# A written order for all five queues from tile 1 on, with attention and weight sums cut into small pieces

## The chip, the cores and the metric

The kernel runs on one core of a Trainium2 chip. TensorE (PE) multiplies matrices into PSUM, VectorE (DVE), ScalarE (ACT) and GpSimd (POOL) work on elements, and SyncE (SP) issues nearly all DMA transfers here. Each engine works through its own queue in order and waits at an instruction until what it needs is there. The metric is the device time of one execution in microseconds; smaller is better.

## The reference

```python
scores = scale * np.matmul(q, k.transpose(0, 1, 3, 2))      # q, k, v: 8 batches, 8 heads, 576 x 64
mask = (rel >= 0) & (rel < window)                           # window = 64
scores = np.where(mask, scores, -1000000000.0)
scores = scores - np.max(scores, axis=-1, keepdims=True)
attn = np.exp(scores)
attn = attn / (np.sum(attn, axis=-1, keepdims=True) + 1e-09)
x = np.matmul(attn, v)                                       # then laid out as 4608 tokens x 512
rms = np.sqrt(np.mean(x * x, axis=-1, keepdims=True) + 1e-06)
xn = x / rms * rms_g
g = xn @ w_gate                                              # 512 x 1536
silu = g * (1.0 / (1.0 + np.exp(-g)))
val = xn @ w_val
return (silu * val @ w_out).astype(np.float32)               # 1536 x 512
```

All arrays are fp32. The kernel keeps the accuracy by splitting each fp32 operand of the large products into an f16 high part and an f16 low part and adding three f16 products (high by high, high by low, low by high).

## The kernel before

The 4608 tokens are nine tiles of 512 (tile 0 to 8). A batch has 576 tokens, so batch b fills the end of one tile and most of the next; its attention is done while the tile before is multiplied. Batches 0 and 1 belong to the start (tile 0, where the weights are also widened and split); the change concerns what follows, batches 2 to 7 and tiles 1 to 8.

**Tiles.** In tiles 1 and 2, `expert_in` makes 24 groups of 12 matmuls of 512 columns (`pg`, `pv`: gate and value), each pair followed by a tanh (L850, ACT), two multiply steps (L851, L852, DVE), the high part (L853, ACT) and the low part (L854). `expert_out` then makes `po`, 24 chunks of 6 matmuls, and `store` copies it out (`ot`, L1046, ACT). From tile 3 on (`FIRST7`) a product of 2 by 2 blocks is done with seven products instead of eight: `seventh` runs product p of chunk c (12 matmuls of 256 columns, L927), at slot 7c + `PLACE[p]` of its tile's 66 slots. The other slots hold `po` chunks. Some of the seven need sums of the activations (`combine`, L785 to L797: `xn`, `wt`, `t`) and of the weights. `snap` (L942, ACT) copies product 1, 5 or 6 away so that later products may add to it on DVE (L980, L983, L987); product 7's sum is made in the copy of product 5 (`p5`, a piece of `wt` in SBUF).

**Weight sums.** `prepare` makes the weights' sums once, in twelve calls, each a block of DVE, ACT, POOL and SP instructions (L878 to L892); the results lie in DRAM (`sevens`), and `load_sevens` (L909, SP) brings a chunk's back before it is used, into a ring of three, after the last product that read the buffer.

**Attention.** A batch has four pairs of heads. For a pair: q and kv are loaded (L325, L340, L353, L354, SP), 36 matmuls give the scores (L396), nine masks with a running maximum (L409, DVE), nine exps with sums (L412, ACT), a reciprocal (L439, L440), a scaling in two multiplies (L373, POOL), a way to DRAM and back that regroups the rows (`via`, L377 and L381, SP), a transpose (L384, L385, DVE), 36 matmuls with the values (L520), copies to `xb` (L577), a square (L583, ACT) and a sum `ssq` (L588). After four pairs the root of the mean square is taken. For batches 0 and 1, `inverse_roots` reduces with columns of one (`tot`, L685), does 11 DVE steps on 128x5 numbers and spreads them with matmuls (`broadcast`, `rb`, L727). From batch 2 on, `roots_of_all` multiplies `ssq` with a matrix of ones (`tot`, L712) and does the same 11 DVE steps on 128 x n numbers, once for each of two pieces. `normalise` then scales `xb` (L752, DVE) and makes `xn` for two tiles.

**What sets the order.** The program is written as a sequence of half-steps, 32 to a tile; events have a time in half-steps and are written when the sequence gets there. `visit(n)` writes the scores of pair n with its whole softmax and the values of pair n-2 at one point (`VISITS`, then every 8 half-steps); the scaling follows 1.5 half-steps later, the transpose 6, and the loads come 7 half-steps before the scores. Tile's scheduler then places each engine's instructions by a simulated timeline of its own, with priorities from the order of writing; only on PE, from chunk 3 of tile 1, does `group()` bind each group to the one written before it. PSUM is in several small pools (`ps_mi`, `ps_x`, `ps_mo` and others) until tile 3, and one pool of eight banks from there.

Of the kernel before, what the change touches and what calls it, by code (L numbers as in the profile page):

```python
# [58 lines left out]
def tile_window_attention_moe(
# [25 lines left out]
    in_order = {"on": False}  # L85

    @contextmanager
    def group():

        if not in_order["on"]:  # L90
            yield
            return
        last = next(x for x in reversed(nc.cur_bb.bb.instructions) if x.engine == nc.tensor.engine)
        with tc.issue_after(last):
            yield
# [434 lines left out]
    def attention(b):  # L530
# [12 lines left out]
        def score(hp, g, first=None):  # L543
            qk = qs[hp], pairs[hp][0]
            if b < TB:
                soft[hp, g] = scores(b * NPAIR + hp, g, qk)
            elif g == 0:
                scores_of_pair(b * NPAIR + hp, qk, first)

        def moved(hp):  # L550
            p, m, rs = whole[b * NPAIR + hp]
            move(b * NPAIR + hp, m, p, rs)

        def turned(hp):
            p, m, _ = whole.pop(b * NPAIR + hp)
            turn(p, m)
            soft[hp, 0] = soft[hp, 1] = p
# [4 lines left out]
        def values(hp, g, xp=None):  # L562
# [19 lines left out]
            if x2e == "a":
                nc.scalar.activation(x2, xb[:, hp, :], AF.Square)  # L583
            else:
                (nc.vector if x2e == "v" else nc.gpsimd).tensor_tensor(x2, xb[:, hp, :], xb[:, hp, :], ALU.mult)
            if hp:
                add = nc.vector if (E('ADD', 'ppvppv')[3 * b + hp - 1] == 'v' if b < 2 else hp == NPAIR - 1) else nc.gpsimd
                add.tensor_tensor(ssq, ssq, x2, ALU.add)  # L588
# [120 lines left out]
    def roots_of_all(b, ssq, a, z):  # L709

        tot = x_bank(f"tot_{b}_{a}")[:, : z - a]
        nc.tensor.matmul(tot, lhsT=ones, rhs=ssq[:, a:z], start=True, stop=True)  # L712
# [501 lines left out]
```

## Time and profile before

| | us |
|---|---|
| median of three runs (1052.85 to 1056.49) | 1053.8 |
| the profiled execution | 1056.1 |
| its span, first to last instruction | 1054.3 |
| PE busy | 972.0 |
| DVE, ACT, POOL busy | 655.8, 507.1, 338.6 |

The mean granted clock of PE is 0.971 of full speed. Times in the profile count from the start of the span. The first product of each tile starts at 58.8 (tile 0), 211.7, 338.4, 454.5, 557.0, 662.1, 770.7, 875.8 and 961.9 us (tile 8). Tiles 1 to 6 have attention beside them, tiles 7 and 8 have none. A row such as "PE pv L802 <- DVE th L851" says that PE, about to write `pv` at line 802, had stood idle until DVE had written `th` at line 851. "L802 PE MATMUL ... [5.44 <-DVE th L851]" puts the same wait before one instruction. PEld is the loading of weights into PE and overlaps with PE. The ends of matmuls are modelled and overlap (a row of 0.38 us is followed by the next after 0.215), so starts are the better ruler.

### The profile page before, as it was taken

The numbers are of one execution on the slowest core, as the hardware profiler recorded it, in microseconds if no ns is written. First come the engines' busy times: TensorE is split into PE (matmuls) and PEld (weight loads), VectorE is DVE, ScalarE is ACT, GpSimd is POOL, SyncE is SP. The second block draws the span as 40 slices with busy tenths as digits, with TensorE's granted clock in tenths as the row PEclk, the third lists the DMA queues.
The fourth block names the chain that finished last, engine by engine and source line by source line (L and its number), as shares of the span: only waits on it lengthen the run. The fifth ranks groups of instructions, "written<-read, shape, count | busy, mean of one in ns | idle before, by whom it ended". The sixth has DMA issues, their size and how long they took to land.

```text
span 1054.3 us, 20343 instructions
## 1 busy us (share of the span) xinstructions
PE 972.0 (92%) x7740; PEld 629.6 (60%) x7751; DVE 655.8 (62%) x1713; ACT 507.1 (48%) x1303; POOL 338.6 (32%) x367
## 2 busy tenths in 40 slices
PE   7789989997989899989898999899989899999998
PEld 5544534553434344478656874687468757866875
DVE  5688856288779634846575766666666566531550
ACT  5557875254434343255535653465345525532541
POOL 3425633245424333323223332433243214210210
PEclk9999989998989999999999999999989999999999
DMA  7647851344541656268645774577436532551601
GB/s 282 192 152 221 262 168 50 116 151 136 171 138 58 196 167 202 71 191 278 226 137 155 260 267 140 151 249 256 155 104 208 163 111 82 198 171 35 206 1 40
DMA packets 78241, 171.72 MB, mean 163 GB/s; under 512 B 25792, under 2 KB 38336, under 8 KB 73536
## 3 DMA queue, kind: packets, MB, share of 16 engines
q1 hardware_dynamic: 77568, 169.24, 50.0%
q8 instruction: 61, 1.00, 0.4%
q10 hardware_dynamic: 576, 1.18, 0.3%
q14 instruction: 36, 0.29, 0.1%
HBM read 135.79 MB, written 34.60 MB: 162 GB/s over the span
## 4 chain that ended last, share of the span: by engine, by line
PE 29%; DMA 11%; DVE 10%; ACT 9%; issue 3%; POOL 3%; SPq 2%; DVEq 0%; ACTq 0%; POOLq 0%
PE a L927 17%; DMA pm<-via 6%; DMA via<-pm 5%; ACT pm L412 5%; PE po L802 4%; PE po L804 4%; PE po L803 4%; POOL pm L373 2%; DVE pm L384 2%; SPq L377 1%; DVE th L952 1%; DVE th L953 1%; ACT h L958 1%; ACT th L951 1%; DVE xb L752 1%
## 5 line engine op out<-in xcount | busy, mean ns | idle before, releaser
L927 PEld LDWEIGHTS <-wt 128*128 128x128 f16 x3024 | 297.2, 98 | 75.3 <-issue 32.9
L927 PE MATMUL a<-xn,wt 128*128 128x256 f16 x1728 | 206.3, 275 | 19.7 <-ACT wt L942 7.9
L802 PE MATMUL po<-wt,h 128*128 128x512 f16 (+1 forms) x436 | 164.8, 378 | 0.0
L804 PE MATMUL po<-wt,h 128*128 128x512 f16 (+1 forms) x436 | 164.6, 377 | 0.0
L803 PE MATMUL po<-wt,h 128*128 128x512 f16 (+1 forms) x436 | 164.6, 377 | 0.0
L959 POOL TENSOR_TENSOR h<-th,h 128x512 f16<-128x512 f32 x60 | 69.6, 1160 | 249.2 <-ACT h L958 241.7
L927 PE MATMUL a<-wt,wt 128*128 128x256 f16 x1104 | 134.9, 275 | 9.3 <-ACT s L942 9.3
L412 ACT ACTIVATE pm<-pm,st 128x128 f32<-128x128 f32 (+1 forms) x216 | 83.1, 387 | 24.3 <-DVE st L409 24.1
L373 POOL TENSOR_TENSOR pm<-pm,st 128x1024 f32<-128x1024 f32 (+1 forms) x48 | 59.2, 1252 | 88.0 <-DVE st L440 59.0
L952 DVE SCALAR_TENSOR_TENSOR th<-th,a 128x256 f32<-128x256 f32 x108 | 45.3, 420 | 62.4 <-ACT th L951 61.9
L958 ACT CAST h<-th 128x512 f16<-128x512 f32 x72 | 44.4, 617 | 79.5 <-DVE th L953 79.5
L384 DVE STREAM_TRANSPOSE pm<-pm 128x1024 f32<-128x1024 f32 x24 | 29.9, 1245 | 72.5 <-DMA pm<-via 60.3
L951 ACT ACTIVATE th<-a,hsc 128x256 f32<-128x256 f32 x108 | 51.3, 475 | 44.6 <-PE a L927 25.5
L804 PEld LDWEIGHTS <-h 128*128 128x128 f16 x436 | 43.0, 99 | 49.7 <-issue 2.2
L802 PE MATMUL pv<-xn,wt 128*128 128x512 f16 x144 | 57.6, 400 | 14.4 <-DVE th L851 14.4
L802 PEld LDWEIGHTS <-h 128*128 128x128 f16 x436 | 43.2, 99 | 46.5 <-issue 2.5
L803 PEld LDWEIGHTS <-h 128*128 128x128 f16 x436 | 43.2, 99 | 46.0 <-issue 3.0
L396 PE MATMUL sc<-kv,q 64*64 64x128 f32 (+1 forms) x1056 | 57.5, 300 | 8.4 <-DMA q<-q 5.0
L803 PEld LDWEIGHTS <-wt 128*128 128x128 f16 x296 | 29.6, 100 | 54.3 <-issue 24.1
L854 POOL TENSOR_TENSOR h<-th,h 128x512 f16<-128x512 f32 x30 | 37.4, 1251 | 69.5 <-ACT h L853 60.5
L802 PE MATMUL pg<-xn,wt 128*128 128x512 f16 x144 | 54.8, 381 | 5.3 <-DVE th L852 3.1
L785 ACT CAST xn<-xb 128x192 f16<-128x192 f32 (+7 forms) x33 | 12.9, 423 | 96.4 <-DVE xb L752 96.2
(189 smaller groups left out, 1780.3 us busy)
## 6 DMA issues: line engine op xcount, KB each, us to landing
wt<-sevens SPq DMA_DIRECT2D x36, 1024.0 KB, 5.9
wt<-sevens SPq DMA_DIRECT2D x36, 768.0 KB, 4.4
kv<-kv SPq DMA_DIRECT2D x28, 608.0 KB, 4.7
via<-pm SPq DMA_DIRECT2D x96, 144.0 KB, 2.8
pm<-via SPq DMA_DIRECT2D x24, 576.0 KB, 4.2
q<-q SPq DMA_DIRECT2D x28, 288.0 KB, 3.1
kv<-kv SPq DMA_DIRECT2D x56, 128.0 KB, 4.8
out<-ot SPq DMA_DIRECT2D x27, 256.0 KB, 2.1
```

Of the source, the lines that this page charges most:

```text
L373: nc.gpsimd.tensor_tensor(p[:, :ks, us, :], p[:, :ks, us, :], r, ALU.mult)
L384: nc.vector.transpose(p[:, :, : NBLK - 1, :], m[:, :, : NBLK - 1, :])
L396: nc.tensor.matmul(out.rearrange("p (n c) -> p n c", c=D), lhsT=qt[hd, j * D : (j + 1) * D], rhs=halves[hd, :1, :] if j == 0 else halves[h ...
L412: nc.scalar.activation(part, part, AF.Exp, bias=low, scale=-1.0, accum_out=total)
L802: nc.tensor.matmul(acc, lhsT=lh, rhs=rh, start=first, stop=False)
L803: nc.tensor.matmul(acc, lhsT=lh, rhs=rl, start=False, stop=False)
L804: nc.tensor.matmul(acc, lhsT=ll, rhs=rh, start=False, stop=last)
L927: nc.tensor.matmul(acc[:, i * HT : (i + 1) * HT], lhsT=ws[l][:, kt, :], rhs=b[:, m, kt, :], start=at_start, stop=kt == 1 and j == 2, skip_ ...
L951: nc.scalar.activation(cols, acc[:, :HT], AF.Tanh, scale=th_scale[:, c : c + 1])
L952: nc.vector.scalar_tensor_tensor(cols, cols, 1.0, acc[:, :HT], ALU.add, ALU.mult)
L958: nc.scalar.copy(hh, th)
L959: (nc.vector if c == NC - 1 else nc.gpsimd).tensor_tensor(hl, th, hh, ALU.subtract)
```

## The change

From tile 1 on, one time scale of slots holds everything: 72 slots for tiles 1 and 2 (`LONG`), 66 for tiles 3 to 8 (`SHORT`); a slot is six matmuls of 512 columns or twelve of 256. `at_slot` keeps a sorted list, and `rest_of_tiles` writes what is due before each slot's matmuls. A pair's softmax is no longer one block: scores at slot -14, -4, 8 or 21 of the tile, masks 0.5 apart, exps 0.9 apart, scaling at 10 (in three multiplies instead of two), to DRAM at 12.5, back at 16, transpose at 22, values at slot 12, 22, 34 or 47 of the tile, then square and sum. Loads are written 6 slots before the scores (14 for the first two pairs). `normalise` and `combine` are lists of pieces 0.85 apart. `prepare` is twelve lists of twelve parts, 0.9 apart, one list every 9.6 slots from slot 3 of tile 1. Roots are those of batches 0 and 1 for all batches (`NRB = B`); `roots_of_all` is gone. Product 7's sum goes into the PSUM bank of product 3. The eight-bank pool begins with tile 1. At the end each instruction written after that point is bound to follow the one written before it on its engine, on all five engines.

```diff
-VISITS = (27, 32, 37, 42.5, 47.5)
-MOVED, TURNED = 1.5, 6
+SCORES, VALUES = (-14, -4, 8, 21), (12, 22, 34, 47)
+LOAD, MASK, EXP, SUM, SCALE, AWAY, BACK, TURN = -6, (0.3, 0.5), (1.3, 0.9), 9.7, 10, 12.5, 16, 22
+ROOTS, FIRST, SECOND, PIECE = 50.5, 52.5, 61, 0.85
 FIRST7 = 3
-SLOTS = 66
 PLACE = {1: 0, 5: 2, 2: 3, 6: 4, 3: 6, 7: 8, 4: 12}
-ORDERED = (1, 3)
-PREP0, PREP1 = 34.0, 72.0
+LONG, SHORT = 72, 66
+PREP, PREP_EVERY, PREP_PIECE = 3, 9.6, 0.9
 ST = 2 * NBLK * P - 32
-NRB = 2
...
+NRB = B
...
+    def scale(p, rs):
+
+        for ks, us in ((4, slice(0, 4)), (4, slice(4, NBLK - 1)), (2, slice(NBLK - 1, NBLK))):
...
+    vias = {}
+
+    def away(n, p):
+        vias[n] = dram.tile([P, 4, NBLK * 32], F32, tag="via", name=f"via_{n}", bufs=3)
...
+    def back(n, m):
+        nc.sync.dma_start(out=m.rearrange("p q j c -> p q (j c)"), in_=vias.pop(n))
...
+        parts = [(MASK[0] + MASK[1] * i, partial(mask, u)) for i, u in enumerate(order)]
+        parts += [(EXP[0] + EXP[1] * i, partial(power, u)) for i, u in enumerate(order)]
+        return parts + [(SUM, invert)]
...
+    def attention_slots(b):
+        load_queries, load_keys, score_pair, moves, values, squares, add, roots, normal_parts = attention(b)
+        t0 = tile_start(b - 1)
+
+        def all_of(hp, when):
+            for off, part in score_pair(hp):
+                at_slot(when + off, part)
+            for off, part in moves(hp):
+                at_slot(when + off, part)
+
+        def normal(piece, when):
+            for i, part in enumerate(normal_parts(piece)):
+                at_slot(when + PIECE * i, part)
+
+        for hp in range(NPAIR):
+            s, v = t0 + SCORES[hp], t0 + VALUES[hp]
+            early_by = 14 if b == TB and hp < 2 else -LOAD
+            at_slot(s - early_by, partial(load_queries, hp))
+            at_slot(s - early_by, partial(load_keys, hp))
+            at_slot(s, partial(all_of, hp, s))
+            at_slot(v, partial(values, hp, 0))
+            at_slot(v + 0.4, partial(values, hp, 1))
+            at_slot(v + 1.5, partial(squares, hp))
+            at_slot(v + 2.2, partial(add, hp))
+        at_slot(t0 + ROOTS, roots)
+        at_slot(t0 + FIRST, partial(normal, 0, t0 + FIRST))
+        at_slot(t0 + SECOND, partial(normal, 1, t0 + SECOND))
...
-    def visit(n):
-
-        xp = x_bank(f"x0_{n}")
-        if n in visits:
-            visits[n][0](any_bank(f"s0_{n}") if shared else ps_mi.tile([P, TT], F32, tag="mi", name=f"s0_{n}"))
-        if n - 2 in visits:
-            visits[n - 2][1](0, xp)
-            visits[n - 2][1](1)
...
-        tot = ps_mi.tile([P, TT], F32, tag="mi", name=f"tot_{b}")
+        tot = any_bank(f"tot_{b}") if shared else ps_mi.tile([P, TT], F32, tag="mi", name=f"tot_{b}")
...
-    def roots_of_all(b, ssq, a, z):
-
-        tot = x_bank(f"tot_{b}_{a}")[:, : z - a]
-        nc.tensor.matmul(tot, lhsT=ones, rhs=ssq[:, a:z], start=True, stop=True)
-        m, r, w = (
-            wk.tile([P, TT], F32, tag="t2k", name=f"r{i}_{b}_{a}", bufs=T2K)[:, : z - a]
-            for i in range(3)
-        )
-        inverse_root(m, r, w, tot)
-        return r
...
-            rb = broadcast(b, r, a, z) if b < NRB else roots_of_all(b, ssq, a, z)
...
+            held["rb"] = broadcast(b, r, a, z)
...
+        return [
+            partial(copies, 0), partial(whole_of, 0), partial(copies, 1), partial(whole_of, 1), partial(sums, 0), partial(sums, 1),
+            partial(half, 0, 1), partial(half, 0, 0), partial(half, 1, 0), partial(half, 1, 1), partial(away, 0), partial(away, 1),
+        ]
...
-            p5 = kept.pop((c, 5))
-            nc.vector.tensor_tensor(p5, acc, p5, ALU.add)
-            quad(t, c, 1, 1, p5)
+            w = kept[c, "w"]
+            nc.vector.tensor_tensor(w, acc, kept.pop((c, 5)), ALU.add)
+            quad(t, c, 1, 1, w)
...
+    def rest_of_tiles():
+        def until(when):
+            while timed and timed[0][0] <= when:
+                timed.pop(0)[2]()
+
+        now = 0
+        for t in range(1, FIRST7):
+            for c in range(NC):
+                for i in range(2):
+                    for m in range(2):
+                        until(now)
+                        group_in(t, c, i, m, any_bank)
+                        now += 2
+                if t == FIRST7 - 1 and c % 2:
+                    at_slot(now, partial(load_sevens, c // 2))
+            for k in range(TT // P):
+                for c in range(NC):
+                    until(now)
+                    out_unit(t, k, c)
+                    now += 1
...
+        for slot in range(now, tile_start(NT)):
+            until(slot)
...
-    for n in range(NPAIR * TB, NPAIR * B + 2):
-        at_step(visit_at(n), partial(visit, n))
+    for b in range(TB, NBR):
+        attention_slots(b)
...
+    def prepared(n, when):
+        for i, part in enumerate(prepare(n // 2, n % 2)):
+            at_slot(when + PREP_PIECE * i, part)
+
     for n in range(2 * NC):
-        at_step(PREP0 + (PREP1 - PREP0) * n / (2 * NC), partial(prepare, n // 2, n % 2))
+        at_slot(PREP + PREP_EVERY * n, partial(prepared, n, PREP + PREP_EVERY * n))
...
+    rest_of_tiles()
+    assert not plan and not timed
+    start = next(k for k in reversed(range(len(traced))) if traced[k] is mark) + 1
+    for ins in traced[start:]:
+        if ins.engine in before and ins.engine in WRITTEN(nc):
+            tc.add_manual_dep(
+                ins, before[ins.engine].name,
+                mybir.DependencyInfo(mybir.DependencyClass.NoSync, mybir.DependencyReason.DATA), reason="written order",
+            )
+        before[ins.engine] = ins
```

Three places show the order. First ACT between tiles 5 and 6. `ot_5_k` are the output copies of tile 5, `pm_30` is the softmax of batch 7's third pair, `xb`, `xn` and `wt` belong to the activations' pieces, and `s1_6_0` is the copy of tile 6's first product. Before:

```order
L412 ACTIVATE pm_30_8216,st_30_8217<-pm_30_8216,st_30_8217 128x2x32
L785 CAST wt1_82<-t1_7_128_8119 128x2x224
L785 CAST wt4_85<-xb_6_6971 128x2x224
L412 ACTIVATE pm_30_8216,st_30_8217<-pm_30_8216,st_30_8217 128x4x32 x7
L785 CAST wt4_85<-t0_7_128_8118 128x2x224
L1046 ACTIVATE ot_5_2_8178<-po_5_2_8139,hsc_123 128x512
L412 ACTIVATE pm_30_8216,st_30_8217<-pm_30_8216,st_30_8217 128x4x32
L785 CAST xn_7_8097<-t2_7_128_8120 128x2x224
L577 COPY xb_7_8248<-x0_30_8194 128x320
L577 COPY xb_7_8248<-xp_28_1_8251 128x256
L942 COPY s1_6_0_8294<-a1_6_0_8281 128x512
```

After (`pm_29` is the pair before it):

```order
L1135 ACTIVATE ot_5_2_8055<-po_5_2_7995,hsc_123 128x512
L827 CAST wt0_81<-t3_6_0_8030 128x2x64
L411 ACTIVATE pm_29_8088,st_29_8089<-pm_29_8088,st_29_8089 128x2x32
L827 CAST wt4_85<-t2_6_0_8061 128x2x64
L411 ACTIVATE pm_29_8088,st_29_8089<-pm_29_8088,st_29_8089 128x4x32 x2
L827 CAST xn_7_8043<-xb_6_7137 128x2x224
L827 CAST xn_6_6769<-t4_6_0_8123 128x2x64
L411 ACTIVATE pm_29_8088,st_29_8089<-pm_29_8088,st_29_8089 128x4x32
L1007 COPY s1_6_0_8159<-a1_6_0_8146 128x512
L827 CAST xn_7_8043<-xb_6_7137 128x2x224
L411 ACTIVATE pm_29_8088,st_29_8089<-pm_29_8088,st_29_8089 128x4x32
L827 CAST xn_7_8043<-xb_6_7137 128x2x224
```

Seven exps of a pair in one row become pieces of one or two between the casts, and the third output copy stands ahead of the pair's exps.

Second DVE where batch 3's root is taken, at the end of tile 2: `ssq_3` is the sum of squares, `tot_3` its sum over features. Before:

```order
L588 TENSOR_TENSOR ssq_3_3396<-ssq_3_3396,kv_15_3433 128x576
L854 TENSOR_TENSOR h_2_5_3982<-th_2_11_4110,h_2_5_3982 128x512
L700 TENSOR_SCALAR r0_3_0_4145<-tot_3_0_4143 128x320
L701 TENSOR_SCALAR r1_3_0_4146<-r0_3_0_4145 128x320
L705 TENSOR_TENSOR r2_3_0_4147<-r1_3_0_4146 128x320
L706 SCALAR_TENSOR_TENSOR r2_3_0_4147<-r2_3_0_4147,r0_3_0_4145 128x320
L707 SCALAR_TENSOR_TENSOR r1_3_0_4146<-r2_3_0_4147,r1_3_0_4146 128x320
L705 TENSOR_TENSOR r2_3_0_4147<-r1_3_0_4146 128x320
L706 SCALAR_TENSOR_TENSOR r2_3_0_4147<-r2_3_0_4147,r0_3_0_4145 128x320
```

After:

```order
L894 SCALAR_TENSOR_TENSOR th_2_11_3987<-pv_2_11_3974,th_2_11_3987 128x512
L896 TENSOR_TENSOR h_2_5_3915<-th_2_11_3987,h_2_5_3915 128x512
L611 TENSOR_TENSOR ssq_3_3482<-ssq_3_3482,kv_15_3540 128x576
L744 TENSOR_SCALAR rm_3_4045<-tot_3_4039 128x5
L745 TENSOR_SCALAR rm_3_4045<-rm_3_4045 128x5
L749 TENSOR_TENSOR rm_3_4045<-rm_3_4045 128x5
L750 SCALAR_TENSOR_TENSOR rm_3_4045<-rm_3_4045 128x5
L751 SCALAR_TENSOR_TENSOR rm_3_4045<-rm_3_4045 128x5
```

The eleven steps on 320 columns (and eleven more on 256 that follow later) become eleven on 5 columns.

Third SP in tile 5, at the loads of two pairs. Before:

```order
L909 DMA wt0_81<-sevens3_131 128x4096
L909 DMA wt0_81<-sevens3_131 128x3072
L325 DMA q_26_6722<-q 128x576
L909 DMA wt1_82<-sevens4_132 128x4096
L377 DMA via_23_6104<-pm_23_5987 32x4x288 x3
L340 DMA kv_24_6065<-kv 128x1216
L353 DMA kv_24_6065<-kv 64x512
L354 DMA kv_24_6065<-kv 64x512
L377 DMA via_23_6104<-pm_23_5987 32x4x288
```

After:

```order
L974 DMA wt0_81<-sevens3_131 128x4096
L974 DMA wt0_81<-sevens3_131 128x3072
L318 DMA q_27_7208<-q 128x576
L333 DMA kv_27_7210<-kv 128x1216
L346 DMA kv_27_7210<-kv 64x512
L347 DMA kv_27_7210<-kv 64x512
L974 DMA wt1_82<-sevens4_132 128x4096
L974 DMA wt1_82<-sevens4_132 128x3072
L374 DMA via_26_7324<-pm_26_7043 32x4x288 x4
```

The queries of pair 26 were written long before the keys of pair 24; now q and kv of one pair, 27, stand together behind the weights' sums of chunk 3, and the four transfers of `via` are no longer parted.

More of the change, by code (lines that the diff above doesn't have):

```diff
@@ L83, in any_bank @@
         return shared["banks"].tile([P, TT], F32, tag="bank", name=name)
[L85 to L95, printed above, removed]
     def x_bank(name):
@@ L541, in load_keys, with score, score_pair, moves @@
             pairs[hp] = load_kv(b * NPAIR + hp)
-        def score(hp, g, first=None):
+        def score(hp, g):
             qk = qs[hp], pairs[hp][0]
[L545 to L557, printed above, removed]
+            soft[hp, g] = scores(b * NPAIR + hp, g, qk)
+        def score_pair(hp):
+            n = b * NPAIR + hp
+            first = any_bank(f"s0_{n}") if shared else ps_mi.tile([P, TT], F32, tag="mi", name=f"s0_{n}")
+            return scores_of_pair(n, (qs[hp], pairs[hp][0]), first)
+        def moves(hp):
+            n = b * NPAIR + hp
+            def turned():
+                p, m, _ = whole.pop(n)
+                turn(p, m)
+                soft[hp, 0] = soft[hp, 1] = p
+            return (
+                (SCALE, lambda: scale(whole[n][0], whole[n][2])),
+                (AWAY, lambda: away(n, whole[n][0])),
+                (BACK, lambda: back(n, whole[n][1])),
+                (TURN, turned),
+            )
         def to_keys(hp, g):
@@ L831, in tile_window_attention_moe, with group_in @@
     held = {}
+    def group_in(t, c, i, m, bank):
+        xn = xn_tiles[t]
+        if (t, c) not in hs:
+            hs[t, c] = h_tile(t, c)
+        f = 2 * c + i
+        fs = slice(i * P, (i + 1) * P)
+        hh, hl = hs[t, c][:, 0, i, :], hs[t, c][:, 1, i, :]
+        w = (wg, wv)[m][c]
+        a = bank(f"p{'gv'[m]}_{t}_{f}")
+        for kt in range(NKD):
+            three(a, w[:, 0, kt, fs], w[:, 1, kt, fs], xn[:, 0, kt, :], xn[:, 1, kt, :], kt == 0, kt == NKD - 1)
+        if m == 0:
+            acc_of[t, f] = a
+            return
+        g = acc_of.pop((t, f))
+        th = wk.tile([P, TT], F32, tag="t2k", name=f"th_{t}_{f}", bufs=T2K)
+        nc.scalar.activation(th, g, AF.Tanh, scale=th_scale[:, c : c + 1])
+        nc.vector.scalar_tensor_tensor(th, th, 1.0, g, ALU.add, ALU.mult)
+        nc.vector.scalar_tensor_tensor(th, a, 2.0**-41, th, ALU.mult, ALU.mult)
+        (nc.vector.tensor_copy if t < 2 and E('HHE', 'a' * 24)[12 * t + f] == 'v' else nc.scalar.copy)(hh, th)
+        (nc.vector if t and c == NC - 1 else nc.gpsimd).tensor_tensor(hl, th, hh, ALU.subtract)
@@ L869, in prepare, with copies @@
         at = 8 * TT + 3 * TT * i
-        for j in range(2):
+        r, halves = [], []
+        names = {}
+        def copies(j):
             part = out_of[:, at + TT * j : at + TT * (j + 1)].rearrange("p (k f) -> p k f", k=NKD)
@@ L1174, in tile_window_attention_moe @@
     late = ctx.enter_context(tc.tile_pool(name="late", bufs=1))
-    all_sevens()
-    assert not plan
+    traced = nc.cur_bb.bb.instructions
+    before = {}
+    for ins in traced:
+        before[ins.engine] = ins
+    mark = traced[-1]
+    rest_of_tiles()
[6 more added lines that the diff above has]
+                mybir.DependencyInfo(mybir.DependencyClass.NoSync, mybir.DependencyReason.DATA), reason="written order",
+            )
+        before[ins.engine] = ins
 def kernel(**inputs):
```

291 lines of the change are left out of this document (141 added, 150 removed).

## The prediction

> **What bounds the kernel now.** I read the engine shares first, then a table of busy time by tile, then what PE waited for, then the rows around the waits.
>
> The page's head and first part:
>
> ```profile
> span 1054.3 us, 20343 instructions
> PE 972.0 (92%) x7740; PEld 629.6 (60%) x7751; DVE 655.8 (62%) x1713; ACT 507.1 (48%) x1303; POOL 338.6 (32%) x367
> ```
>
> PE is the bound, so the question is when it stands still or runs slowly. Busy time by stretch, cut where a tile's first product starts (window, length; busy time of PE, PEld, DVE, ACT, POOL; PEclk; DMA share, GB/s). The rows are tiles 1 to 7:
>
> ```profile
> 211.70:338.40 126.70, 113.89 (x805) 55.41 (x802) 104.27 (x248) 54.16 (x165) 52.34 (x51) 0.95 0.43 132
> 338.40:454.50 116.10, 106.44 (x726) 51.86 (x725) 68.40 (x187) 49.78 (x152) 41.24 (x43) 0.98 0.51 162
> 454.50:557.00 102.50, 97.64 (x928) 73.44 (x928) 65.73 (x171) 46.48 (x127) 28.77 (x31) 0.97 0.62 203
> 557.00:662.10 105.10, 97.92 (x942) 72.48 (x941) 68.81 (x194) 53.10 (x155) 34.35 (x38) 1.00 0.61 206
> 662.10:770.70 108.60, 99.75 (x942) 72.94 (x941) 72.61 (x201) 54.14 (x158) 35.04 (x39) 0.98 0.60 196
> 770.70:875.80 105.10, 96.89 (x797) 69.86 (x796) 64.84 (x153) 49.21 (x123) 31.96 (x33) 0.95 0.45 143
> 875.80:961.90 86.10, 86.10 (x649) 63.38 (x648) 37.60 (x71) 34.52 (x62) 18.82 (x16) 1.00 0.44 144
> ```
>
> Tile 7, which has no attention beside it, is full: 86.10 us, clock 1.00. Its 66 slots make one slot 86.10/66 = 1.305 us. Tiles 1 to 6 take 664.1 us together and PE is busy for 612.5 of them, so 51.6 us are gaps. No engine but PE is near full over a tile; DVE in tile 1 comes nearest (104.27 of 126.7). What ended PE's gaps in tiles 1 to 6 (total us, times, longest):
>
> ```profile
> PE pv L802 <- DVE th L851: 10.8, 4, 5.4
> PE a L927 <- ACT s L942: 9.3, 3, 3.6
> PE tot L712 <- DVE ssq L588: 8.2, 4, 4.8
> PE a L927 <- ACT wt L942: 7.9, 7, 3.1
> PE a L927 <- DVE wt L987: 6.0, 4, 3.0
> PE a L927 <- ACT ot L1046: 3.2, 1, 3.2
> ```
>
> These 45.4 us are few, long waits for short steps that stood late in the queue of ACT or DVE. ACT's timeline shows such a queue at the start of tile 3 (start, length):
>
> ```profile
> 449.52 0.39 ACT L412 ACTIVATE pm<-pm,st 128x128 f32<-128x128 f32 x1
> ...
> 453.18 0.67 ACT L583 ACTIVATE ssq<-xb 128x576 f32<-128x576 f32 x1
> 453.75 0.67 ACT L1046 ACTIVATE ot<-po,hsc 128x512 f32<-128x512 f32 x1
> ```
>
> From 449.52 to 453.18 ACT does exps with little between, then a square, and only then the copy that frees the bank PE waits 3.2 us for.
>
> The clock comes on top. Three stretches around gaps:
>
> ```profile
> 254.00:262.00 8.00, 3.85 (x10) 1.34 (x10) 6.79 (x7) 3.83 (x9) 6.65 (x5) 0.62 0.48 135
> 521.00:530.00 9.00, 5.99 (x89) 4.99 (x87) 6.77 (x27) 4.39 (x14) 0.15 (x1) 0.81 0.75 272
> 562.00:568.00 6.00, 3.76 (x29) 2.65 (x28) 1.93 (x5) 5.16 (x13) 4.04 (x5) 1.00 0.39 92
> 258.15 0.58 PE L802 MATMUL pv<-xn,wt 128*128 128x512 f16 x1 [5.44 <-DVE th L851]
> 524.25 1.49 PE L927 MATMUL a<-xn,wt 128*128 128x256 f16 x12 [3.01 <-DVE wt L987]
> 564.67 1.47 PE L927 MATMUL a<-wt,wt 128*128 128x256 f16 x12 [2.24 <-ACT s L942]
> ```
>
> The gaps of 5.44 and 3.01 us come with a lower clock, the one of 2.24 does not. By the tile rows the clock costs (1-0.95)x126.7 + 0.02x116.1 + 0.03x102.5 + 0 + 0.02x108.6 + 0.05x105.1 = 19.2 us.
>
> **What PE must do there.** One pair's scores and values, on PE (start, length):
>
> ```profile
> 444.84 0.27 PE L396 MATMUL s<-kv,q 64*64 64x64 f32 x2
> ...
> 446.60 0.64 PE L520 MATMUL xp<-pm,kv 128*64 128x64 f32 x16
> 447.17 0.39 PE L802 MATMUL po<-wt,h 128*128 128x512 f16 x1
> ```
>
> That is 447.17-444.84 = 2.33 us, 24 times, less one pair's scores (0.95, the start of L520 at 445.79) that fall into tile 0: 55.0. Tiles 1 and 2 have 72 slots, 3 to 6 have 66: 2x72x1.305 + 4x86.10 = 532.3. Roots today are one kind of row and become another:
>
> ```profile
> L712 PE MATMUL tot<-ssq,one 128*128 128x384 f32 (+7 forms) x24 | 8.9, 455 | 8.2 <-DVE ssq L588 8.2
> 192.88 1.17 PE L685 MATMUL tot<-one,ssq 128*128 128x1 f32 x10
> 203.13 1.00 PE L727 MATMUL rb<-ident,rm 128*128 128x128 f32 x8
> 210.26 0.66 PE L727 MATMUL rb<-ident,rm 128*128 128x64 f32 x4
> 194.09 0.16 DVE L700 TENSOR_SCALAR rm<-tot 128x5 f32<-128x5 f32 x1 [4.65 <-PE tot L685]
> 196.08 0.17 DVE L707 SCALAR_TENSOR_TENSOR rm<-rm 128x5 f32<-128x5 f32 x1
> L705 DVE TENSOR_TENSOR r<-r 128x384 f32<-128x384 f32 x6 | 3.3, 558 | 0.2
> ```
>
> 532.3 + 55.0 + 8.9 = 596.2, and with 19.2 for the clock 615.4 against 612.5 measured: the account closes within 3 us.
>
> **The change, part by part.**
>
> 1. Roots as batch 1 has them. PE pays 1.17+1.00+0.66 = 2.83 per batch, 17.0 for six, against 8.9: a loss of 8.1. DVE gets 11 steps in 2.2 us (194.09 to 196.25) for two pieces of 11 steps at up to 0.56: about 10 us of DVE per batch go, which PE sees only through the waits of part 2.
>
> 2. Written order, small pieces, `prepare` spread over nearly two tiles. The least that PE can then take is 532.3+55.0+17.0 = 604.3, so at most 664.1-604.3 = 59.8 can be gained. What remains I estimate from how much PE work the new order puts between a producer and its user, in slots of 1.305:
>  - `tot` stands 2.5 slots (3.3 us) behind the last values. The way there is copy, square (0.67), sum and three hand-overs, some 3.3 to 4: 0.5 us x 6. From `tot` to `rb` 2 slots (2.6) cover 2.2 of DVE: 0.3 x 6. Together 5.
>  - First chunk of tiles 3 to 6: the copies of `snap` have 2 to 3 slots; adding the rows' durations, ACT has up to 13 us of work in the 13 us there, as exps, casts and tanh still meet. 1 us each instead of today's 2.2 to 3.6: 4.
>  - Tiles 1 and 2: `prepare` keeps DVE at up to 13 us in 13; 2.
>  - The bank switch moves from tile 3 to tile 1, where the first `pg` follows the last copy of tile 0 with nothing between: like today's 3.2.
>  - Clock, for those that last long enough: 3.
>  - Late q or kv (below): 3.
>
>  Together 20. The ends: 0 where every cover holds, 50 where the waits only change places.
>
> 3. q and kv are asked for 6 slots (7.8 us) before the scores, not 7 half-steps of a tile (7/32 of 102 to 127 us, 22 to 28). Landing times (median us), and what SP waited for before it could load keys (total, times, longest):
>
> ```profile
> kv<-kv SPq DMA_DIRECT2D x28, 608.0 KB, 4.7
> q<-q SPq DMA_DIRECT2D x28, 288.0 KB, 3.1
> kv<-kv SPq DMA_DIRECT2D x56, 128.0 KB, 4.8
> SPq L340 <- DVE ssq L588: 31.8, 6, 8.5
> ```
>
>  Four transfers issued one behind the other land in some 6.5 us by these medians, so about 1 us is left. I take 0.5 us for each of the six pairs whose load stands right behind a reload of the weights' sums: 3. The ends are 0 and the rival C.
>
> 4. p7's sum into the PSUM bank instead of SBUF, eight banks from tile 1, three multiplies in place of two on POOL (32% busy): 0. The cover is that each bank is reused two slots or more after its last reader; if it goes, it is a wait of one copy, 0.6 us.
>
> 5. Tile 0, 7 and 8: the same work; 0.
>
> Sum: 664.1 becomes 604.3+20 = 624, a gain of about 40. With the 3 us by which the account is too high, 43. The profiled execution took 1056.1 (span 1054.3), 2.3 above the median of the runs, 1053.8. So 1056.1-43-2.3 gives 1011 on the scale of the median.
>
> On the clock, the Trainium skill (TensorE: Matmul & The Clock Gate, Part 1: The HAM clock gate) says that PE falls to half rate only after an idle window of about 3.4 us. The gap of 2.24 us agrees with it; the one of 3.01 us lost clock though it is shorter, and here the trace decides. By the page's figure the gaps left above would cost no clock, and the time would be 1008, as an estimate.
>
> **Rivals.**
>
> A. Nearly all waits go: residue about 5, the gain 58, 996. For it: tile 7 shows PE without any gap, with the same products and copies. Against it: tile 7 has no exps, and ACT at a tile's start has no room.
>
> B. The waits change place. All queues are now fixed, so a step that waits holds everything behind it. Two rows:
>
> ```profile
> DVE pm L384 <- DMA pm<-via: 60.3, 19, 5.7
> SPq L909 <- PE a L927: 196.5, 53, 8.2
> ```
>
> DVE stood 60.3/19 = 3.2 us in front of a transpose; the way back now has 6 slots (7.8 us) from its issue, and SP can be held 196.5/53 = 3.7 in front of it. If 24 transposes hold DVE so and PE loses 1 us each, 24, with the clock 0 to 8 more: the gain falls to 11 to 19, 1035 to 1043, about 1040. Against it: the hold was there before too, and mask, exp and transpose of different pairs are now apart.
> The Trainium skill (same page, Part 1) calls the queues of ScalarE and VectorE strict FIFO, which is this mechanism; the 60.3 us agree.
>
> C. Slower: the scores wait for q and kv. If SP waits for a kv buffer as in the row of L340, 31.8/6 = 5.3 us, then 6.5+5.3-7.8 = 4.0 us for 22 pairs (the first two keep 14 slots): 88, so 43-88 = 45 slower, 1099. It decides from 43/22 = 2.0 us a pair, a landing of 9.8 us. Against it: in the new order the value matmuls and the sum that free a buffer stand at least a slot and a half ahead of its next load.
>
> D. The order on the engines barely moves the waits, or gains equal the dearer roots: 1050 to 1057.
>
> **How the numbers follow.** Chances: forecast 0.50 (1002 to 1022), A 0.22, B 0.15, C 0.08, D 0.05. The range goes from just under A (992) to within B's upper end (1042) and leaves out C, D and a little of A and B. A change under 0.3%, 3 us, can't be told from none: D gives 0.04 same; slower is C and a part of D, 0.09; the rest, 0.87, is faster.
>
> **What would show it.** After the change: tiles 3 to 6 of 98 to 102 us (86.1+4x2.33+2.83 = 98.2 at the least) and tiles 1 and 2 of 105 to 111; gaps after L851, `snap` copies and `ssq` of under 1.5 us each; PEclk 0.98 or more in each tile; one gap at the start of tile 1 of 1 to 3 us. I am wrong if scores wait for DMA (C), if `pm<-via` is the chain's main part with PE waiting for DVE behind it (B), or if the added PE work of the roots is far from 8 us.

## The result, and the profile after

The changed kernel takes 1002.5 us (median of four runs, 1002.08 to 1004.02) against 1053.6 for the kernel before: a ratio of 0.9513, 95% interval 0.9492 to 0.9533, or 51 us less. The forecast was 1011 in a range of 992 to 1042. The profiled execution took 1004.0.

The page's head and first part after:

```profile
span 1002.1 us, 20583 instructions
PE 971.0 (97%) x7853; PEld 632.1 (63%) x7853; DVE 578.4 (58%) x1647; ACT 498.9 (50%) x1303; POOL 330.3 (33%) x391
```

PE is busy as long as before (972.0), in a span 52 us shorter. The rows of tiles 1 to 6, cut at each tile's first product as before, and the sum of the six:

```profile
212.10:320.70 108.60, 106.86 (x740) 52.64 (x740) 74.06 (x189) 46.17 (x133) 40.81 (x41) 1.00 0.47 131
320.70:427.90 107.20, 106.84 (x743) 52.94 (x742) 63.91 (x176) 46.30 (x136) 42.79 (x50) 1.00 0.63 196
427.90:525.30 97.40, 97.40 (x945) 72.58 (x944) 57.41 (x182) 52.30 (x157) 31.45 (x39) 1.00 0.70 229
525.30:625.50 100.20, 100.20 (x960) 73.96 (x959) 58.79 (x184) 52.58 (x156) 33.55 (x42) 1.00 0.66 213
625.50:725.40 99.90, 99.90 (x957) 73.71 (x956) 58.93 (x184) 52.55 (x156) 33.61 (x42) 1.00 0.65 217
725.40:823.20 97.80, 97.78 (x888) 72.20 (x887) 54.43 (x146) 47.87 (x130) 32.07 (x38) 1.00 0.57 191
sum 611.10, PE 608.99 PEld 398.03 DVE 367.54 ACT 297.77 POOL 214.29; mean PE 101.50 PEld 66.34 DVE 61.26 ACT 49.63 POOL 35.71
```

664.1 us have become 611.1, all of the gain. The gaps fell from 51.6 to 2.1, and the granted clock is 1.00 in every tile. What the clock had cost can now be read from the same matmuls: from start to start and without gaps, the products and `po` of these tiles took 548.4 us before and 535.5 after, so some 13 us. Against this stand the roots (6.9 before, 13.2 after) and the scores and values (57.1 and 60.4): 49.5 + 12.9 - 6.3 - 3.3 = 52.8. All that PE still waits for in these six tiles:

```profile
PE tot L729 <- DVE ssq L611: 1.7, 1, 1.7
PE pg L845 <- ACT ot L1135: 0.6, 1, 0.6
PE s L395 <- DMA kv<-kv: 0.4, 1, 0.4
```

PE waits for no copy of `snap` any more. ACT stands ready instead: at the start of tiles 4, 5 and 6 it waits some 2.9 us for the first product. The row of ACT's own waits over tiles 3 to 6, and below it DVE's wait in front of the transposes over tiles 1 to 6, 60.3 us in 19 waits before:

```profile
ACT s L1007 <- PE a L992: 8.8, 3, 3.0
DVE pm L383 <- DMA pm<-via: 0.7, 1, 0.7
```

The root's matmuls in tiles 1 to 6 (the busy times of rows overlap, so from start to start they are 13.2 us, against 6.9 for L712 before):

```profile
L729 PE MATMUL tot<-one,ssq 128*128 128x1 f32 x60 | 7.1, 244 | 1.7 <-DVE ssq L611 1.7
L760 PE MATMUL rb<-ident,rm 128*128 128x128 f32 x42 | 6.6, 278 | 0.0
L760 PE MATMUL rb<-ident,rm 128*128 128x64 f32 x24 | 4.0, 248 | 0.0
```

### The profile page after: what moved, and what is told of

It is laid out like the page before. It is cut to its first block, busy times and chain, and to the rows that moved or that the text cites. A ratio compares the mean times of both kernels' runs of the same rounds, so it can differ in the third digit from the quotient of the medians.

```text
span 1002.1 us, 20583 instructions
## 1 busy us (share of the span) xinstructions
PE 971.0 (97%) x7853; PEld 632.1 (63%) x7853; DVE 578.4 (58%) x1647; ACT 498.9 (50%) x1303; POOL 330.3 (33%) x391
## 4 chain that ended last, share of the span: by engine, by line
PE 70%; DMA 1%; ACT 0%; SPq 0%; DVE 0%; issue 0%; DVEq 0%; ACTq 0%
PE a L992 33%; PE po L845 8%; PE po L847 8%; PE po L846 8%; PE xp L526 3%; PE sc L395 2%; PE pg L845 1%; PE pv L845 1%; PE pv L847 1%; PE pv L846 1%; PE pg L847 1%; PE pg L846 1%; PE rb L760 1%; PE tot L729 1%; DMA kv<-kv 1%; PE s L395 0%
## 5 line engine op out<-in xcount | busy, mean ns | idle before, releaser
L992 PEld LDWEIGHTS <-wt 128*128 128x128 f16 x3024 | 292.7, 98 | 42.0 <-issue 1.4
L992 PE MATMUL a<-xn,wt 128*128 128x256 f16 x1728 | 205.2, 273 | 0.0
L845 PE MATMUL po<-wt,h 128*128 128x512 f16 (+1 forms) x436 | 162.9, 374 | 0.0
L847 PE MATMUL po<-wt,h 128*128 128x512 f16 (+1 forms) x436 | 162.8, 373 | 0.0
L846 PE MATMUL po<-wt,h 128*128 128x512 f16 (+1 forms) x436 | 162.8, 373 | 0.0
L992 PE MATMUL a<-wt,wt 128*128 128x256 f16 x1104 | 133.7, 273 | 0.0
L1017 DVE SCALAR_TENSOR_TENSOR th<-th,a 128x256 f32<-128x256 f32 x144 | 60.5, 420 | 107.4 <-ACT th L1016 107.4
L1016 ACT ACTIVATE th<-a,hsc 128x256 f32<-128x256 f32 x144 | 67.9, 472 | 91.3 <-DVE a L1045 43.4
L1135 ACT ACTIVATE ot<-po,hsc 128x512 f32<-128x512 f32 (+1 forms) x37 | 25.0, 675 | 148.7 <-PE po L847 128.6
L366 POOL TENSOR_TENSOR pm<-pm,st 128x512 f32<-128x512 f32 (+1 forms) x72 | 59.8, 858 | 50.7 <-DVE st L442 37.1
L828 POOL TENSOR_TENSOR xn<-xb,xn 128x192 f16<-128x192 f32 (+7 forms) x33 | 24.0, 741 | 126.0 <-ACT xn L827 125.7
L1018 DVE SCALAR_TENSOR_TENSOR th<-a,th 128x256 f32<-128x256 f32 x144 | 61.1, 424 | 4.9
L395 PE MATMUL sc<-kv,q 64*64 64x128 f32 (+1 forms) x1056 | 54.7, 295 | 7.6 <-DMA q<-q 4.9
L1045 DVE TENSOR_TENSOR a<-a,s 128x512 f32<-128x512 f32 x36 | 25.0, 695 | 61.9 <-PE a L992 61.5
```

The lines of the kernel that those rows point to most:

```text
L395: nc.tensor.matmul(out.rearrange("p (n c) -> p n c", c=D), lhsT=qt[hd, j * D : (j + 1) * D], rhs=halves[hd, :1, :] if j == 0 else halves[h ...
L845: nc.tensor.matmul(acc, lhsT=lh, rhs=rh, start=first, stop=False)
L846: nc.tensor.matmul(acc, lhsT=lh, rhs=rl, start=False, stop=False)
L847: nc.tensor.matmul(acc, lhsT=ll, rhs=rh, start=False, stop=last)
L992: nc.tensor.matmul(acc[:, i * HT : (i + 1) * HT], lhsT=ws[l][:, kt, :], rhs=b[:, m, kt, :], start=at_start, stop=kt == 1 and j == 2, skip_ ...
L1016: nc.scalar.activation(cols, acc[:, :HT], AF.Tanh, scale=th_scale[:, c : c + 1])
```

## The experiments

Since the change does several things at once, the question was which of them removed the waits. Theory 1: the binding of the queues. Theory 2: the small pieces. Theory 3: the relief of DVE by the new roots. Ratios are to the kernel before on the same chip; the change itself has 0.9513. The new slot times and the eight banks from tile 1 are in all kernels here that start from the change, and were not tested apart.

**Nothing bound.**

```diff
-    return [getattr(nc, e).engine for e in CFG.get("W", ("tensor", "vector", "scalar", "gpsimd", "sync"))]
+    return [getattr(nc, e).engine for e in ()]
```

> The changed kernel with its slots, pieces, pools and roots, but no engine bound to the written order: the scheduler places all five queues again. If the binding of the queues is what removed the waits (theory 1), many of the 51.6 us of gaps in tiles 1 to 6 return and the time is 1025 to 1050. If the small pieces on one time scale did it (theory 2), writing alone is enough: 1002 to 1010, with PE gaps of under 8 us in tiles 1 to 6.

Measured: 1039.0 us, ratio 0.9837 (0.9789 to 0.9886), by which it is 17 us under the kernel before. The six tiles and the main waits of PE:

```profile
sum 646.60, PE 620.11 PEld 403.99 DVE 359.94 ACT 299.47 POOL 219.13; mean PE 103.35 PEld 67.33 DVE 59.99 ACT 49.91 POOL 36.52
PE a L992 <- DVE st L408: 9.3, 4, 2.8
PE a L992 <- ACT s L1007: 5.8, 4, 2.2
```

The gaps are 26.5 us again. ACT in tile 4, where PE waited 1.79 us for the copy `s`, and DVE just before:

```profile
551.02 1.25 DVE L383 STREAM_TRANSPOSE pm<-pm 128x1024 f32<-128x1024 f32 x1 [5.81 <-DMA pm<-via]
552.89 0.47 ACT L1016 ACTIVATE th<-a,hsc 128x256 f32<-128x256 f32 x1 [7.19 <-DVE a L1048]
553.26 0.58 ACT L1007 COPY s<-a 128x512 f32<-128x512 f32 x1
```

The scheduler put a tanh ahead of the copy; the tanh had to wait 7.19 us for DVE, and the copy with it. DVE had itself stood for 5.81 us in front of a transpose whose data were not back from DRAM. Of the ten waits of PE over 1 us in these tiles, seven come within 5 us behind such a stand of DVE (5.1 to 6.3 us each). Writing small pieces isn't enough.

**PE alone bound.**

```diff
-    return [getattr(nc, e).engine for e in CFG.get("W", ("tensor", "vector", "scalar", "gpsimd", "sync"))]
+    return [getattr(nc, e).engine for e in ("tensor",)]
```

> As the changed kernel, but only PE is bound to the written order (before, PE was the only engine bound too). Theory 1: what ACT, DVE, POOL and SP do in front of PE decides, so 1015 to 1045, with PE waiting for ACT and DVE. Theory 2: 1002 to 1010. If it equals the run without any binding, PE's own order is not the point; if it equals the changed kernel, PE's order alone was.

Measured: 1044.3 us, ratio 0.9887 (0.9856 to 0.9919): no better than nothing bound. The waits are of the same kind, and DVE's stands in front of transposes are there too (81.3 us in 14 waits, 68.8 in 14 with nothing bound):

```profile
PE a L992 <- DVE st L408: 9.5, 4, 2.7
PE a L992 <- ACT s L1007: 6.4, 6, 3.1
```

**DVE and ACT alone bound.**

```diff
-    return [getattr(nc, e).engine for e in CFG.get("W", ("tensor", "vector", "scalar", "gpsimd", "sync"))]
+    return [getattr(nc, e).engine for e in CFG.get("W", ("vector", "scalar"))]
```

> The changed kernel with only DVE and ACT bound to the written order; PE, POOL and SP are left to the scheduler, which places POOL nearly as written and some of PE's groups elsewhere. If the order of DVE and ACT is what the binding brings (theory), 1001 to 1010. If PE's or POOL's is needed as well, 1015 to 1040, as with nothing bound or PE alone bound.

Measured: 1017.1 us, ratio 0.9655 (0.962 to 0.969), 36 of the 51 us, and within the second range, that PE's or POOL's order is needed as well. DVE's stands in front of transposes are gone. What is left shows in the sum and in PE's waits:

```profile
sum 627.50, PE 615.58 PEld 400.66 DVE 367.67 ACT 299.89 POOL 214.20; mean PE 102.60 PEld 66.78 DVE 61.28 ACT 49.98 POOL 35.70
PE s L395 <- DMA kv<-kv: 5.0, 3, 2.0
PE rb L760 <- DVE rm L751: 4.4, 3, 2.3
```

With PE free, the scheduler takes `rb` and some scores sooner than they are ready. DVE and ACT are the larger part, PE or POOL the rest; which of those two wasn't told apart. (SP was free here too; the next run shows that this alone costs nothing.)

**All but SP bound.**

```diff
-    return [getattr(nc, e).engine for e in CFG.get("W", ("tensor", "vector", "scalar", "gpsimd", "sync"))]
+    return [getattr(nc, e).engine for e in CFG.get("W", ("tensor", "vector", "scalar", "gpsimd"))]
```

> The changed kernel with PE, DVE, ACT and POOL bound to the written order and SP left to the scheduler. With nothing bound it was 1.6% under the kernel before, with all bound 4.9%. If the order of the transfers on SP is a main part (theory: a load late behind another transfer holds the scores), 1015 to 1040 with waits of PE for kv or the weights' sums. If the order of ACT and DVE is the part that counts, 1002 to 1010.

Measured: 1002.5 us, ratio 0.9494 (0.9471 to 0.9517), as with all five, though SP's queue is ordered otherwise at many places. With the other four bound, the binding of SP is not part of the gain.

**All pieces in one row each.**

```diff
-LOAD, MASK, EXP, ... = -6, (0.3, 0.5), (1.3, 0.9), ...
+LOAD, MASK, EXP, ... = -6, (0.3, 0), (1.3, 0), ...
-ROOTS, FIRST, SECOND, PIECE = 50.5, 52.5, 61, 0.85
+ROOTS, FIRST, SECOND, PIECE = 50.5, 52.5, 61, 0
-PREP, PREP_EVERY, PREP_PIECE = 3, 9.6, 0.9
+PREP, PREP_EVERY, PREP_PIECE = 3, 9.6, 0
```

> The changed kernel with all five queues still bound, but masks, exps, the pieces of normalise and combine, and the twelve parts of each prepare are written in one row each (their spacing set to 0). Theory 2: nine exps in a row hold ACT for 4.4 us and a prepare holds DVE for 6 to 7 us again, more than the 2.6 to 3.9 us that PE has between a producer and its user: gaps return, 1020 to 1050. Theory 1: the fixed order is enough, 1002 to 1012.

Measured: 1043.5 us, ratio 0.9871 (0.9816 to 0.9926). By the ratios, the fixed order without the pieces is worth 14 us, the pieces without the order were worth 17, both together 51. What PE waits for is not what theory 2 named, the steps on ACT or DVE, but the keys:

```profile
PE s L395 <- DMA kv<-kv: 18.7, 6, 4.7
PE xp L526 <- DVE pm L384: 5.9, 3, 4.5
```

One of these waits can be followed through three queues (ACT, SP's issues, PE; start, length):

```profile
526.90 0.41 ACT L827 CAST xn<-xb 128x256 f16<-128x256 f32 x1 [7.79 <-DVE xb L788]
...
531.12 0.68 ACT L1135 ACTIVATE ot<-po,hsc 128x512 f32<-128x512 f32 x1
531.70 0.33 ACT L411 ACTIVATE pm<-pm,st 128x64 f32<-128x64 f32 x1
...
535.11 0.67 ACT L1135 ACTIVATE ot<-po,hsc 128x512 f32<-128x512 f32 x1
531.82 4.33 SPq L1148 DMA_DIRECT2D out<-ot  x3
536.20 0.42 SPq L318 DMA_DIRECT2D q<-q  x1
536.72 0.41 SPq L333 DMA_DIRECT2D kv<-kv  x1
541.90 0.33 PE L395 MATMUL s<-kv,q 64*64 64x64 f32 x4 [3.67 <-DMA kv<-kv]
```

ACT stands in front of the casts of normalise until 526.90, and an output copy behind their row starts at 531.12. Nine exps then hold ACT until 535.11, and the next output copy stands behind them. SP's output transfer waits for that copy, the load issued at 536.2 stands behind SP's transfer, and PE waits at the scores for the keys. At this place the two copies start 8.9 and 11.5 us after the square of the batch's last pair (L603) in the changed kernel, and 12.7 and 16.7 us here.

**Masks and exps alone in one row.**

```diff
-... = -6, (0.3, 0.5), (1.3, 0.9), ...
+... = -6, (0.3, 0), (1.3, 0), ...
```

> The changed kernel with only masks and exps of a pair in one row again. With all three lumps it lost about 40 us. In its trace the nine exps (531.70 to 535.2) stood ahead of an output copy, SP stood behind that copy, and the load of the next keys behind SP. If the exps are the lump that counts (theory 2a), 1020 to 1040 and most of the waits are of scores for kv. If it is the lumps of normalise and prepare (2b), 1002 to 1012.

Measured: 1005.5 us, ratio 0.9545 (0.9508 to 0.9582); the interval holds the change's own 0.9513. The row of exps that I had blamed costs little by itself: at the place shown above the two copies start 8.9 and 12.9 us after the square, and with the rest alone in one row (the next run) 12.7 and 14.0. So there the row of casts was the larger part of the hold. PE waits once for keys:

```profile
PE s L395 <- DMA kv<-kv: 1.7, 1, 1.7
```

**The rest alone in one row.**

```diff
-ROOTS, FIRST, SECOND, PIECE = 50.5, 52.5, 61, 0.85
+ROOTS, FIRST, SECOND, PIECE = 50.5, 52.5, 61, 0
-PREP, PREP_EVERY, PREP_PIECE = 3, 9.6, 0.9
+PREP, PREP_EVERY, PREP_PIECE = 3, 9.6, 0
```

> The counterpart: masks and exps in small pieces, but the pieces of normalise and combine and the parts of each prepare in one row. Theory 2b: 1020 to 1040, and the loss lies mainly in tiles 1 and 2, where prepare holds DVE and SP. Theory 2a: 1002 to 1015.

Measured: 1034.4 us, ratio 0.9821 (0.9783 to 0.986). Tiles 1, 5 and 6, where most of it is lost (108.60, 99.90 and 97.80 with the pieces), and the wait that leads:

```profile
208.10:328.70 120.60, 111.69 (x740) 55.32 (x740) 74.36 (x184) 48.31 (x138) 41.71 (x46) 0.94 0.43 122
637.90:746.20 108.30, 102.35 (x957) 75.20 (x956) 60.83 (x184) 53.12 (x156) 34.24 (x42) 0.97 0.61 200
746.20:853.10 106.90, 99.72 (x887) 73.50 (x886) 57.37 (x165) 49.41 (x137) 32.70 (x41) 0.97 0.56 180
PE s L395 <- DMA kv<-kv: 17.7, 4, 7.2
```

Normalise, combine and prepare are the pieces that matter: 12 us in tile 1 and 4 in tile 2, where prepare runs, and 8 and 9 in tiles 5 and 6, where only normalise and combine do. That the loss would lie mainly in tiles 1 and 2 was wrong; half of it lies behind them. Again PE waits mainly for keys. In tile 5 the way to them is another: POOL scales a pair only from 639.57 us on, behind its own row of normalise and combine, SP sends `via` at 642.0 and asks for the keys at 647.6, and PE has waited 5.8 us for them at 654.36.

**Loads two slots later.**

```diff
-LOAD, ... = -6, ...
+LOAD, ... = -4, ...
```

> The changed kernel with q and kv written 4 slots before the scores instead of 6. In its trace SP asks 6.1 to 16.6 us ahead, and the landing leaves less than 1 us for about half of the 22 pairs. If that cover is as thin as it looks (theory: rival C is near), 2 slots or 2.6 us less bring some 1.5 to 2.6 us for about 12 pairs, 20 to 30 us, and PE waits for kv: 1020 to 1035. If SP, which runs ahead of the slots, sets the time of asking, 1002 to 1006.

Measured: 1013.4 us, ratio 0.9627 (0.9589 to 0.9666), about 11 us more than with 6 slots:

```profile
PE s L395 <- DMA kv<-kv: 9.6, 8, 1.8
```

Eight pairs wait where none had waited over 0.4. The cover is as thin as the trace said, but the price is half of what I expected: SP asks ahead of the written slot, 5.4 to 10.8 us before the scores in this trace (one pair 23), where 4 slots are 5.2.

**All lumps, loads three slots earlier.**

```diff
-LOAD, MASK, EXP, ... = -6, (0.3, 0), (1.3, 0), ...      (the kernel with all lumps)
+LOAD, MASK, EXP, ... = -9, (0.3, 0), (1.3, 0), ...
```

> The kernel with all lumps and with the loads written 9 slots ahead instead of 6. If the lumps hurt by way of SP (the load stands behind an output copy that stands behind the lump), 3.9 us more of lead takes the 18.7 us of waits for kv and the clock lost with them away: 1010 to 1025, 20 to 30 below the run with lumps. If they hurt by holding ACT and DVE in front of PE, it stays at 1035 to 1047.

Measured: 1023.2 us, ratio 0.9714 (0.9681 to 0.9746), against 0.9871. An earlier load alone gives some 16 us of the 38 that the lumps cost back:

```profile
PE s L395 <- DMA kv<-kv: 8.7, 4, 3.2
PE xp L526 <- DVE pm L384: 6.6, 4, 4.5
```

So a good part of the lumps' harm, some two fifths by this run, runs through SP and the keys, by a wait in front of a load, not through ACT or DVE directly. The rest was not told apart.

**The new roots alone, in the kernel before.**

```diff
-NRB = 2
+NRB = B
-        tot = ps_mi.tile([P, TT], F32, tag="mi", name=f"tot_{b}")
+        tot = any_bank(f"tot_{b}") if shared else ps_mi.tile([P, TT], F32, tag="mi", name=f"tot_{b}")
```

(the same for `rb`)

> The kernel before with one part of the change alone: roots on 128x5 numbers for all batches. If the relief of DVE is a main cause (theory 3), the waits for ssq and for L851 shrink and it is 1030 to 1045 in spite of some 8 us more PE work. By theories 1 and 2 the other waits stay: at best the 8.2 us of waits for ssq go against 8.1 us of dearer matmuls, so 1048 to 1060.

Measured: 1059.4 us, ratio 1.0042 (1.0011 to 1.0072): slower by 4 us. The wait for `ssq`, 8.2 us before, grew:

```profile
PE tot L685 <- DVE ssq L588: 23.5, 5, 8.7
```

DVE's relief brings nothing here: PE comes to `tot` before the sum of squares is done, five times. Why the scheduler places it so was not followed up.

**The old roots, in the changed kernel.**

```diff
-            norm["r"] = inverse_roots(b, norm["ssq"])
+            if b < 2:
+                norm["r"] = inverse_roots(b, norm["ssq"])
+            else:
+                norm["r"] = roots_of_all(b, norm["ssq"], 0, TT * (b + 1) - S * b), norm["ssq"]
-            held["rb"] = broadcast(b, r, a, z)
+            held["rb"] = broadcast(b, r, a, z) if b < 2 else roots_of_all(b, r[1], a, z) if piece else r[0]
```

(and `roots_of_all` put back; lines from there on stand 13 further down, so L1005 is the L992 of the change)

> The changed kernel with the roots of before: the first piece's where the new ones stand, the second's at the start of its piece. Tiles 1 to 6 now have PE busy throughout, so only PE's own work counts there: the matmuls of the roots fall from 13.2 us (starts to starts) to some 6.5, and if the 11 DVE steps of up to 0.6 us stay hidden (theory PE work), 994 to 998. If they hold DVE for up to 6.5 us in front of the steps that PE waits for (theory DVE relief: the dearer matmuls buy shorter waits), gaps return: 1005 to 1030.

Measured: 1013.9 us, ratio 0.9608 (0.9581 to 0.9635), some 11 us slower than the change (and than the kernel with SP unbound, 1002.5 on the same chip), though PE has 7 us less to do. What PE waits for, and a row of POOL:

```profile
PE s L395 <- DMA kv<-kv: 7.5, 3, 3.1
PE a L1005 <- ACT s L1020: 4.1, 4, 1.8
PE s L395 <- DVE t L853: 3.3, 1, 3.3
726.63 3.02 POOL L366 TENSOR_TENSOR pm<-pm,st 128x512 f32<-128x512 f32 x3 [9.95 <-DVE st L442]
```

The eleven long DVE steps are a lump too. Once they hold DVE from 719.18 to 726.2; the reciprocal of a softmax (`st`) stands behind them, POOL's scaling behind that, then SP's transfers of `via` and the load of the next keys (734.27), and PE has waited 2.66 us for these keys at 741.95. So the same part loses 4 us in the old order and is worth 11 in the new. That its gain is hidden in the old order because other waits end last there is likely, and was not shown.

**Product 7's sum in SBUF, two multiplies.**

```diff
-            w = kept[c, "w"]
-            nc.vector.tensor_tensor(w, acc, kept.pop((c, 5)), ALU.add)
-            quad(t, c, 1, 1, w)
+            p5 = kept.pop((c, 5))
+            nc.vector.tensor_tensor(p5, acc, p5, ALU.add)
+            quad(t, c, 1, 1, p5)
-        for ks, us in ((4, slice(0, 4)), (4, slice(4, NBLK - 1)), (2, slice(NBLK - 1, NBLK))):
+        for ks, us in ((4, slice(0, NBLK - 1)), (2, slice(NBLK - 1, NBLK))):
```

> The changed kernel with product 7's sum in SBUF and the scaling in two multiplies on POOL, as before the change. The prediction priced both at 0: 1001 to 1005. If the earlier release of the weights' buffer or the shorter hold of POOL mattered, 1006 to 1020, with PE waiting for the weights' sums or for DVE.

Measured: 1002.0 us, ratio 0.9487 (0.9466 to 0.9507), beside 1002.5 for the kernel with SP unbound on the same chip: no effect. No version stands clearly below the changed kernel.

## Why the prediction was right, and where its numbers were off

**The account of the time before held in kind.** The excess over PE's own work lay in gaps and clock of tiles 1 to 6, and all of the gain came from there. That its sum closed within 3 us was partly luck: the clock cost about 12.9 us, not 19.2, and L712 6.9 from start to start, not 8.9, while products and `po` take 535.5, not 532.3, and scores and values took 57.1, not 55.0. Together these are the 3 us.

**Step 2, the residue, was the term that was mis-sized.** I left 20 us. Measured: 2.1 us of gaps (2.7 by the rows of waits) and no lost clock. Piece by piece: `tot` and `rb` 5 forecast, 1.7 measured (once, in tile 1); copies at tile starts 4, no wait in the rows; prepare in tiles 1 and 2, 2 against no wait for its steps; the bank switch 3.2, measured 0.6; clock 3, 0; keys 3, 0.4. What failed there is the reading of ACT at a tile's start: adding up rows, I took it for full, with up to 13 us of work in 13, and so for lagging. In the trace after, ACT is busy for 8.0 to 8.6 us of the first 13 of tiles 3 to 6, and at the start of tiles 4, 5 and 6 it waits for PE. ACT had such waits before too (6.9 us in four), but then PE also waited for copies; now ACT is free when the first product of these tiles ends.

**The least time of PE was 4.7 us too low**: 604.3 forecast, 609.0 busy. The roots are 13.2 by starts, not 17.0. The other way, scores and values take 60.4 us from start to start, where I had 55.0. What remains, 609.0-13.2-60.4 = 535.4, is 3.1 over my 532.3 for products and `po`. One pair at 2.33 us stood for all; why the others take longer was not followed up. So the 39.8 of the sum (664.1 to 624.3) became 39.8 + 17.9 - 4.7 = 53.0. The 3 us that I had added for the error of the account had no ground: PE's own work, from which the gain was reckoned, was too low and not too high.

**Step 1** was right that the roots' price on PE is a loss by itself (6.3 us from start to start, 8.1 forecast; in the kernel before the time rose by 4, with longer waits for `ssq` in it), and wrong to treat DVE's relief as a detail of step 2: undoing it costs 11 us.

**Step 4** (0) is confirmed for product 7 and the multiplies; the eight banks from tile 1 were not tested apart. **Step 3** had the right danger and the wrong lead: SP asks 6.1 to 16.6 us ahead in the trace after (for one pair 39), not 7.8, and the four transfers take 5.9 to 12.1 us, not 6.5. About half of the pairs keep less than 1 us. The pair of these two rows has 6.85 us, and its keys land 6.4 us after the first issue:

```profile
512.14 0.54 SPq L318 DMA_DIRECT2D q<-q  x1
518.99 0.27 PE L395 MATMUL s<-kv,q 64*64 64x64 f32 x2
```

**Rivals.** A (996) named the mechanism better than the forecast did: nearly all waits go. The time lies 8.5 us under the forecast and 6.5 over A, since PE's own work is larger than both assumed. B feared that fixed queues would make DVE stand in front of transposes. The opposite came: these waits fell from 60.3 us to 0.7, and they are long only where the scheduler orders DVE. That a wait holds all behind it is real, as the kernels with lumps show (1034 to 1044, near B's time), but there through SP and the keys. The Trainium skill (TensorE: Matmul & The Clock Gate, Part 1: The HAM clock gate) calls the queues of ScalarE and VectorE strict FIFO; the copy that waited behind a tanh for 7.19 us agrees. C did not come, but its cover is less than two slots: with the loads 4 slots ahead it begins. D is excluded.

## What to carry to other kernels

When the busiest engine has gaps from short steps that stand late in another queue, cutting the work into pieces and fixing the order help most together: here 17 and 14 us apart, 51 together (each with the new slot times and roots). Look for the long row of work that stands in front of a transfer's issue, as the wait comes out two or three queues later, at an engine that never touched it. And test a part in the order in which it will run: the same roots cost 4 us in one and saved 11 in the other.

## What the runs showed of the hardware

**The clock.** Over all profiles I looked at each gap of PE of more than 1.65 us in tiles 1 to 6 for a lower clock within 4 us behind it. Of 20 gaps of 3.41 us and more, all had one; of 11 from 3.0 to 3.4, 8; of 22 from 2.0 to 3.0, 11; of 20 below 2.0, 2. Two that go against a fixed length, of the kernel with exps in one row (a gap of 1.73 us, clock 0.79 over the 8 us) and of the one with old roots (3.09 us, clock 1.00):

```profile
286.71 0.49 PE L729 MATMUL tot<-one,ssq 128*128 128x1 f32 x3 [1.73 <-DVE ssq L611]
284.50:292.50 8.00, 6.27 (x29) 3.45 (x27) 4.24 (x14) 0.84 (x2) 1.15 (x1) 0.79 0.73 227
```

```profile
330.43 0.33 PE L395 MATMUL s<-kv,q 64*64 64x64 f32 x4 [3.09 <-DMA kv<-kv]
325.77:329.18 3.41, 1.56 (x8) 0.49 (x5) 2.32 (x4) 1.45 (x3) 3.03 (x3) 1.00 1.00 303
329.18:332.59 3.41, 2.17 (x41) 1.52 (x42) 0.00 (x0) 0.00 (x0) 2.06 (x4) 1.00 0.98 307
```

The slow stretches last 3.41 us or two or three times that. The Trainium skill (TensorE: Matmul & The Clock Gate, Part 1: The HAM clock gate) has a free-running window of that length, which agrees, and advises against idle gaps longer than about 3.4 us; by these counts a gap of 2 to 3 us loses the clock about every second time. How much of one window is idle tells the two kinds apart far better. In each trace every change of the clock lies within 2 ns of a multiple of 3.413 us from the first one, so the traces can be cut into these windows. In this part of the 14 traces, 2683 windows ran at full clock. In 38 of them PE was idle for 2.0 us or more, and all 38 were followed by a slow window. Of the 63 with 1 to 2 us, 4 were, and three of these also hold the ten matmuls of `tot`, of one column each, for another 1.1 us. Of the other 2582, none was. Both rows fit: the gap of 3.09 us falls into two windows, as 1.85 and 1.24 us (the last two rows above), and that of 1.73 lies with 1.17 us and the matmuls of `tot` in one. This is read from the traces at hand; no kernel was made to test it.
